# A backward pass with an S4 layer and a gated feed-forward net: parameter-gradient blocks with finer due times, their stores on GpSimd's queue, and the input gradient stored from ScalarE's queue

## The chip, the cores and the metric

The kernel runs on one core of a Trainium2 chip. The metric is the device time of one execution in microseconds (us). A core has five engines with a queue of instructions each: TensorE (PE, with its weight loads shown apart as PEld), VectorE (DVE), ScalarE (ACT), GpSimd (POOL) and SyncE (SP). A queue is worked in order, so an instruction that waits holds up all behind it. SP, ACT and POOL also issue DMA transfers between DRAM and the on-chip memory (SBUF); in the profile such issues carry the names SPq, ACTq and POOLq.

## The reference

The forward function normalises `A_u` (2048 rows of 576 channels) and feeds the result to two branches, an S4 convolution and a SwiGLU net with 4608 hidden channels; the output combines them. The kernel returns the output and the gradients of all inputs.

```python
x = A_u
xn = _layernorm(x, axis=-1)
s = _A_ref(xn, A_re, A_im, B_re, B_im, C_re, C_im, log_dt, Dskip)   # S4 convolution
g = _silu(_B_ref(xn, B_w1, B_w3, B_w2))                             # gated net
return x + s * g
...
dt = exp(log_dt); logdA = dt * (A_re + 1j * A_im); dB = dt * (B_re + 1j * B_im)
K[d, l] = real(sum_n C[d, n] * exp(logdA[d, n] * l) * dB[d, n])     # kernel of the convolution
y = irfft(rfft(pad(u)) * rfft(pad(K))) + u * Dskip
```

Outputs 0 and 1 are the result and the gradient of `A_u` (2048 x 576); outputs 2 to 7 are the gradients of A, B and C, real and imaginary parts (576 x 128 each); output 8 is the gradient of `log_dt` (576 numbers), output 9 that of `Dskip`; 10 to 12 are the weight gradients of the net.

## The kernel before

The program is one straight line of instructions for each engine. The forward pass comes first; `backward` (L1126) lays out the rest in stages that overlap: the backward convolution (`ssm_bwd_conv`), the parameter gradients (`ssm_bwd_params`, then `phase5_final`), the weight gradients of the net in 18 groups (`phase6_group`), and last the input gradient (`phase6_inputs`).

**What sets the order.** A planner writes the queue of each engine when the program is built. `at(us)` (L83) gives the instructions that follow a due time; when several instructions of an engine could run, the planner puts the one with the earliest due time first. It works with its own estimates of when things are ready, and once written the order is fixed. Buffers of a pool are reused in turn: a tile from a pool with three buffers waits until the tile three before it has been read for the last time. In `backward` the numbers are T0 = 700, TG = 36, TQ = 75, TC = 14, TX = 18, so the input gradient's tile i is due at 1348 + 18 i.

**Parameter gradients.** `param_chunk` (L1016) works through 36 chunks of 16 channels: PE multiplies into PSUM tiles `et_ps` (L1026), DVE multiplies by `pz` (L1033) and reduces into `S_all` (L1037). Its loads are issued on SP (L1008, L1013, and the transposing load at L1178). `phase5_final` (L1041) then takes the 576 channels in five blocks of 128 (the last has 64). For each block PE transposes four pieces of `S_all` (L1056), ACT copies them to `ST` (L1058), and DVE computes `W` (L314 to L321), `grho` and `gth` (L1067 to L1073), the sums for the gradient of `log_dt` (L1081 to L1097), and the gradients of B and C (L1101 to L1106). Six results of a block are scaled into tiles `gout` (L1076, L1108, L1111), of which there are three buffers, and stored with `self.dma` (L77, the issue itself is L81), which takes SP and ACT in turn. The memory of this step is that of the chunks' buffers, so it begins when the last chunk is done. After the last block the sums go out to output 8 in two stores on SP (L1119, L1121): the first writes 512 numbers of 2 bytes one by one, since neighbouring numbers lie in different partitions.

**Input gradient.** `phase6_inputs` (L1287) takes 16 tiles of 128 rows. For each tile SP loads two transposed operands, `ggc` and `guc` (L1178), which have two buffers each; PE runs 144 matmuls (L1316) into two PSUM halves `px`, also with two buffers; DVE adds the convolution's part into `gx` (L1326), which frees `px`; then `ln_bwd_tile` (L1356) takes the gradient through the layer norm on ACT (L1365) and DVE (L1368 to L1377), and the result `o1` is stored by `self.dma` (L1379), on SP and ACT in turn. ACT also issues the loads of `gxs` and `go` (L1322, L1324).

Of the kernel before, what the change touches and what calls it, by code (L numbers as in the profile page):

```python
# [16 lines left out]
P = 128  # L17
# [43 lines left out]
class K:  # L61
# [840 lines left out]
    def ssm_bwd_params(self, T0, TC, T2, S_all, ps):  # L902
        cfg = self.cfg
        D, LT = cfg.D, cfg.LT
        with self.tc.tile_pool(name="g_k", bufs=1, side="right") as gkp, self.tc.tile_pool(name="g_q", bufs=2, side="right") as qp:
            gz = []
            for i in range(3):
                z = gkp.tile([P, 2, 2, 2, 16, LT], BF16, name=f"gz{i}")
                self.nc.gpsimd.memset(z[:], 0.0)
                gz.append(z)  # L910
            NCH = D // 16
            AHEAD = 2
            q = []
            when = lambda c: T0 + TC * c + (40 if T0 + TC * c > T2 - 30 else 0)
            for ch in range(NCH + AHEAD):
                if ch < NCH:
                    self.at(when(ch - AHEAD))
                    q.append(self.param_load(ch, gz[ch % 3], qp))
                if ch >= AHEAD:
                    self.at(when(ch - AHEAD))  # L920
                    self.param_chunk(ch - AHEAD, q.pop(0), S_all, qp, ps)
# [119 lines left out]
    def phase5_final(self, out, big, S_all, ps2, T, TX):  # L1041
        nc, cfg = self.nc, self.cfg
        D, DT, N = cfg.D, cfg.DT, cfg.N
# [3 lines left out]
        pp = out.enter_context(self.tc.tile_pool(name="gfp", bufs=1, side="right"))  # L1047
        if True:
            self.load_rates(pp)
            glogdt = big.tile([P, DT], FP32, name="glogdt")  # L1050
            nc.vector.memset(glogdt[:], 0.0)
            for c, (do, dsz) in enumerate(cfg.dch):
                self.at(T + TX * c)
                pt = ps2.tile([P, 4, N], FP32, name="et_ps")
                for kd in range(4):
                    nc.tensor.transpose(pt[0:dsz, kd, :], S_all[:, kd, do:do + dsz], self.ident_f[:])  # L1056
                ST = fp.tile([P, 4, N], FP32, name="ST")
                nc.scalar.copy(out=ST[0:dsz], in_=pt[0:dsz])  # L1058
                v = slice(0, dsz)
                S1r, S2r, S1i, S2i = ST[v, 0, :], ST[v, 1, :], ST[v, 2, :], ST[v, 3, :]  # L1060
                Wr_t, Wi_t = self.compute_W(fp, c, dsz)
                Wr, Wi = Wr_t[v], Wi_t[v]
                dtc = self.dt_col[v, c:c + 1]
                grho = fp.tile([P, N], FP32, name="grho")
                gth = fp.tile([P, N], FP32, name="gth")
                t1 = fp.tile([P, N], FP32, name="ft1")
                nc.vector.tensor_tensor(out=grho[v], in0=Wr, in1=S2r, op=ALU.mult)  # L1067
                nc.vector.tensor_tensor(out=t1[v], in0=Wi, in1=S2i, op=ALU.mult)
                nc.vector.tensor_tensor(out=grho[v], in0=grho[v], in1=t1[v], op=ALU.subtract)
                nc.vector.tensor_tensor(out=gth[v], in0=Wr, in1=S2i, op=ALU.mult)  # L1070
                nc.vector.tensor_tensor(out=t1[v], in0=Wi, in1=S2r, op=ALU.mult)
                nc.vector.tensor_tensor(out=gth[v], in0=gth[v], in1=t1[v], op=ALU.add)
                nc.vector.tensor_scalar(out=gth[v], in0=gth[v], scalar1=-1.0, scalar2=None, op0=ALU.mult)  # L1073
                for src, oname in ((grho, "out_2"), (gth, "out_3")):
                    ob = fo.tile([P, N], BF16, name="gout")
                    nc.vector.tensor_scalar(out=ob[v], in0=src[v], scalar1=dtc, scalar2=None, op0=ALU.mult)  # L1076
                    self.dma(aps[oname][do:do + dsz, :], ob[v])
                acc1 = fp.tile([P, 1], FP32, name="acc1")
                acc2 = fp.tile([P, 1], FP32, name="acc2")
                junk = fp.tile([P, N], FP32, name="junk")  # L1080
                nc.vector.tensor_tensor_reduce(out=junk[v], in0=grho[v], in1=self.A_re[v, c, :], scale=1.0, scalar=0.0,  # L1081
                                               op0=ALU.mult, op1=ALU.add, accum_out=acc1[v])
                nc.vector.tensor_tensor_reduce(out=junk[v], in0=gth[v], in1=self.A_im[v, c, :], scale=1.0, scalar=0.0,
                                               op0=ALU.mult, op1=ALU.add, accum_out=acc2[v])
                nc.vector.tensor_tensor(out=acc1[v], in0=acc1[v], in1=acc2[v], op=ALU.add)
                acc3 = fp.tile([P, 1], FP32, name="acc3")
                acc4 = fp.tile([P, 1], FP32, name="acc4")
                nc.vector.tensor_tensor_reduce(out=junk[v], in0=S1r, in1=Wr, scale=1.0, scalar=0.0,
                                               op0=ALU.mult, op1=ALU.add, accum_out=acc3[v])
                nc.vector.tensor_tensor_reduce(out=junk[v], in0=S1i, in1=Wi, scale=1.0, scalar=0.0,  # L1090
                                               op0=ALU.mult, op1=ALU.add, accum_out=acc4[v])
                nc.vector.tensor_tensor(out=acc3[v], in0=acc3[v], in1=acc4[v], op=ALU.subtract)
                rdt = fp.tile([P, 1], FP32, name="rdt")
                nc.vector.reciprocal(out=rdt[v], in_=dtc)
                nc.vector.tensor_tensor(out=acc3[v], in0=acc3[v], in1=rdt[v], op=ALU.mult)
                nc.vector.tensor_tensor(out=acc1[v], in0=acc1[v], in1=acc3[v], op=ALU.add)
                nc.vector.tensor_tensor(out=glogdt[v, c:c + 1], in0=acc1[v], in1=dtc, op=ALU.mult)  # L1097
                for (Xr, Xi, on_r, on_i) in ((self.B_re, self.B_im, "out_6", "out_7"), (self.C_re, self.C_im, "out_4", "out_5")):
                    gr = fp.tile([P, N], FP32, name="gr")
                    gi_ = fp.tile([P, N], FP32, name="gi")  # L1100
                    nc.vector.tensor_tensor(out=gr[v], in0=S1r, in1=Xr[v, c, :], op=ALU.mult)  # L1101
                    nc.vector.tensor_tensor(out=t1[v], in0=S1i, in1=Xi[v, c, :], op=ALU.mult)
                    nc.vector.tensor_tensor(out=gr[v], in0=gr[v], in1=t1[v], op=ALU.subtract)
                    nc.vector.tensor_tensor(out=gi_[v], in0=S1r, in1=Xi[v, c, :], op=ALU.mult)
                    nc.vector.tensor_tensor(out=t1[v], in0=S1i, in1=Xr[v, c, :], op=ALU.mult)
                    nc.vector.tensor_tensor(out=gi_[v], in0=gi_[v], in1=t1[v], op=ALU.add)  # L1106
                    ob = fo.tile([P, N], BF16, name="gout")
                    nc.vector.tensor_scalar(out=ob[v], in0=gr[v], scalar1=dtc, scalar2=None, op0=ALU.mult)  # L1108
                    self.dma(aps[on_r][do:do + dsz, :], ob[v])
                    ob2 = fo.tile([P, N], BF16, name="gout")  # L1110
                    nc.vector.tensor_scalar(out=ob2[v], in0=gi_[v], scalar1=dtc, scalar2=-1.0, op0=ALU.mult, op1=ALU.mult)  # L1111
                    self.dma(aps[on_i][do:do + dsz, :], ob2[v])
            gl_bf = big.tile([P, DT], BF16, name="gl_bf")
            nc.vector.tensor_copy(out=gl_bf[:], in_=glogdt[:])
            nfull = D // P
            rem = D - nfull * P
            with nc.allow_non_contiguous_dma(reason="small vector store"):
                if nfull > 0:
                    nc.sync.dma_start(out=aps["out_8"][0:nfull * P].rearrange("(c p) -> p c", p=P), in_=gl_bf[:, 0:nfull])  # L1119
                if rem > 0:  # L1120
                    nc.sync.dma_start(out=aps["out_8"][nfull * P:D].rearrange("(p o) -> p o", o=1),  # L1121
                                      in_=gl_bf[0:rem, nfull:nfull + 1])
# [3 lines left out]
    def backward(self, T0, TG, TQ, TC, TX, gctx, mats):  # L1126
        nc, cfg = self.nc, self.cfg
        D, L, LT, F, FT = cfg.D, cfg.L, cfg.LT, cfg.F, cfg.FT
# [8 lines left out]
        with ExitStack() as out:  # L1137
# [7 lines left out]
            ps = out.enter_context(pool(name="b_ps", bufs=3, space=PS, side="right"))  # L1145
# [6 lines left out]
            T1 = T0 + 4 * TQ  # L1152
            self.ssm_bwd_params(T1, TC, T2, S_all, ps)
            self.at(T1 + TC * D // 16)
            self.phase5_final(out, fix, S_all, ps, T1 + TC * D // 16, TX)
            cur = self.phase6_load(0, T0 - TG, TG, wp, inp)
            for gi in range(NG):
                nxt = self.phase6_load(gi + 1, T0 + TG * gi, TG, wp, inp) if gi + 1 < NG else None
# [197 lines left out]
    def ln_bwd_tile(self, sb, sm, gx, i, go_t):  # L1356
# [19 lines left out]
        o1 = sb.tile([P, D], BF16, name="o1")  # L1376
        nc.vector.scalar_tensor_tensor(out=o1[:], in0=u[:], scalar=self.rstd[:, i:i + 1], in1=go_t[:],  # L1377
                                       op0=ALU.mult, op1=ALU.add)
        self.dma(out1[i * P:(i + 1) * P, :], o1[:])  # L1379


# [99 lines left out]
```

## Time and profile before

| | |
|---|---|
| median of 13 runs | 2059.11 us (2043.48 to 2103.01) |
| profiled execution | 2061.33 us, of which the span from first to last instruction is 2059.6 us |
| PE busy | 1789.9 us, 87% of the span |
| DVE busy | 1501.9 us, 73% |
| ACT busy | 968.4 us, 47% |
| POOL busy | 510.1 us, 25%; none after 1684 us |
| mean granted TensorE clock | 0.958 |

Times in the profile count from the span's start. The chain that ended last is followed back from the last instruction: each step is the work, or the wait, that released the next one. In a timeline, a bracket after a line tells how long the engine had been idle and what released it. The granted clock is the share of full speed that TensorE was allowed. `gout`, `o`, `gl_bf` and so on are the program's tile names with numbers left out (`out_dram` stands for any output).

### The profile page before, as it was taken

To read this page: it belongs to the slowest core of one execution; us is meant where nothing else is said; L and a number is where in the kernel's file an instruction comes from. 1 tells how busy PE (TensorE), PEld (TensorE's weight loads), DVE (VectorE), ACT (ScalarE), POOL (GpSimd) and SP (SyncE) were. 2 spreads that over 40 slices of the span, in tenths; PEclk is the share of its full clock that TensorE was granted. 3 is DMA by queue.
4 is the path that set the end of the run, shared out by engine and by line. 5 is a ranking of instruction groups with operands and counts; after the bars stand their busy time and mean duration, and the time that the engine had idled before them with its cause. 6 is when DMAs were issued, how large, how long until landed. Compare 5 with 4: busy or idle time off the path is not lost. (4 is left out here: it accounts for less than half of the span.)

```text
span 2059.6 us, 40511 instructions
## 1 busy us (share of the span) xinstructions
PE 1789.9 (87%) x16214; PEld 1246.7 (61%) x16214; DVE 1501.9 (73%) x2616; ACT 968.4 (47%) x1733; POOL 510.1 (25%) x682
## 2 busy tenths in 40 slices
PE   2888988989899699989999999897996994899985
PEld 1443333335454477777777777675775773677764
DVE  7459999998783456569695878586995865388681
ACT  1968888886456311474747565343543410000000
POOL 6016566662123011212122212322231210000000
PEclk9899999999999899999999999998998997999998
DMA  6678788877578998646463645999889899999773
GB/s 174 242 271 291 272 281 276 280 266 256 181 265 197 197 208 189 181 125 175 135 204 115 191 142 155 235 242 210 228 204 166 216 216 192 196 218 231 169 146 41
DMA packets 551981, 421.29 MB, mean 205 GB/s; under 512 B 415472, under 2 KB 482224, under 8 KB 547184
## 3 DMA queue, kind: packets, MB, share of 16 engines
q1 hardware_dynamic: 488096, 254.56, 52.0%
q0 software_dynamic: 39056, 147.49, 22.5%
q10 hardware_dynamic: 24640, 16.65, 3.2%
q8 instruction: 127, 2.08, 0.4%
q14 instruction: 62, 0.51, 0.1%
HBM read 135.96 MB, written 196.27 MB: 161 GB/s over the span
## 5 line engine op out<-in xcount | busy, mean ns | idle before, releaser
L1033 DVE TENSOR_TENSOR pr_q<-et_ps,pz 128x512 f32<-128x512 f32 x288 | 186.6, 684 | 77.1 <-PE et_ps L1026 70.3
L1272 PEld LDWEIGHTS <-xn_bf 128*128 128x128 bf16 x2304 | 224.3, 98 | 29.6 <-issue 2.9
L768 PEld LDWEIGHTS <-xnT 128*128 128x128 bf16 x1152 | 101.6, 98 | 168.6 <-issue 71.8
L1037 DVE TENSOR_REDUCE S_all<-pr_q 128x16 f32<-128x1024 f32 x144 | 175.1, 1216 | 2.1
L1225 PE MATMUL ph<-w2T,goT 128*128 128x256 bf16 x1152 | 173.1, 281 | 2.0 <-DVE e L840 2.0
L1253 PE MATMUL pgw<-go_o,h_n 128*128 128x288 bf16 x1152 | 163.7, 292 | 0.0
L768 PE MATMUL pg<-wmB_w,xnT 128*128 128x512 bf16 x576 | 160.2, 387 | 2.9 <-ACT g_t L777 2.0
L1316 PEld LDWEIGHTS <-guc 128*128 128x128 bf16 x1152 | 114.4, 100 | 77.3 <-DMA guc<-GU_dram 28.0
L1365 ACT ACTIVATE t<-gx 128x576 f32<-128x576 f32 x16 | 10.9, 683 | 314.6 <-DVE gx L1326 262.4
L768 PE MATMUL pu<-wmB_w,xnT 128*128 128x512 bf16 x576 | 152.7, 382 | 0.0
L499 POOL COPY pz_k<-p_k 128x256 bf16<-128x256 bf16 x144 | 138.7, 1006 | 46.6 <-issue 37.1
L831 PE MATMUL po<-w2g,hc 128*128 128x288 bf16 x1152 | 147.5, 291 | 1.3 <-ACT u_t L778 1.3
L1274 ACT CAST gw<-pgw 128x256 bf16<-128x256 f32 x144 | 54.5, 379 | 197.3 <-PE pgw L1272 196.5
L1316 PEld LDWEIGHTS <-ggc 128*128 128x128 bf16 x1152 | 114.6, 100 | 42.5 <-DMA ggc<-GG_dram 12.2
L1272 PE MATMUL pgw<-gu_n,xn_bf 128*128 128x256 bf16 x1152 | 132.9, 272 | 1.6 <-ACT gw L1257 1.1
L1316 PE MATMUL px<-wTA,guc 128*128 128x288 bf16 x512 | 110.5, 298 | 26.6 <-DMA guc<-GU_dram 26.6
L831 PEld LDWEIGHTS <-hc 128*128 128x128 bf16 x1152 | 113.2, 99 | 32.6 <-issue 1.7
L1253 PEld LDWEIGHTS <-h_n 128*128 128x128 bf16 x1152 | 112.7, 100 | 28.6
L1272 PE MATMUL pgw<-gg_n,xn_bf 128*128 128x256 bf16 x1152 | 129.4, 273 | 0.0
L1225 PEld LDWEIGHTS <-goT 128*128 128x128 bf16 x1152 | 101.6, 100 | 44.4 <-issue 14.8
L1316 PE MATMUL px<-wTA,ggc 128*128 128x288 bf16 x512 | 110.9, 297 | 17.9 <-DMA ggc<-GG_dram 12.1
L1228 ACT CAST gh<-ph 128x512 bf16<-128x512 f32 x144 | 82.2, 604 | 81.7 <-PE ph L1225 51.6
(321 smaller groups left out, 4179.8 us busy)
## 6 DMA issues: line engine op xcount, KB each, us to landing
G_dram<-g_t POOLq DMA_DIRECT2D x72, 256.0 KB, 4.0
U_dram<-u_t POOLq DMA_DIRECT2D x72, 256.0 KB, 3.6
H_dram<-h_t SPq DMA_DIRECT2D x72, 256.0 KB, 3.4
Q_dram<-q_k SPq DMA_DIRECT2D x36, 512.0 KB, 3.4
gg_n<-G_dram POOLq DMA_DIRECT2D x18, 1024.0 KB, 5.8
h_n<-U_dram POOLq DMA_DIRECT2D x18, 1024.0 KB, 8.3
GU_dram<-gu_n POOLq DMA_DIRECT2D x72, 256.0 KB, 4.3
GG_dram<-gg_n POOLq DMA_DIRECT2D x72, 256.0 KB, 5.6
```

The source lines that it names most:

```text
L499: nc.gpsimd.tensor_copy(out=pz[:, g, h, 1:3], in_=pv[:, g, h])
L768: nc.tensor.matmul(pt[:], lhsT=xnT[:, c, ts], rhs=wm[w][:, c, :], start=(c == 0 and not first), stop=(c == nfull - 1 and first))
L831: nc.tensor.matmul(po_[:, pi_, 0:pw], lhsT=hc[:, fi, :], rhs=w2[fi][:, po:po + pw], start=(fi == 0), stop=(fi == FT - 1))
L1033: nc.vector.tensor_tensor(out=pr[:, r].rearrange("p k m a -> p m k a"), in0=T[h][:, r][:, None].to_broadcast([P, 2, 4, 2, AV]), in1=pz[:, ...
L1037: nc.vector.tensor_reduce(out=S_all[:, :, d0:d0 + 4].rearrange("p (s k) d -> p k s d", k=2), in_=pr[:].rearrange("p r k (s d) a -> p k s d ...
L1225: nc.tensor.matmul(ph[j][:, k, :], lhsT=lw, rhs=rh, start=(n == 0), stop=(n == nfull))
L1228: nc.scalar.copy(out=gh[:, j], in_=ph[j][:])
L1253: nc.tensor.matmul(pgw[pi_][:, 0:pw], lhsT=hn[:, tt, fl * P:(fl + 1) * P], rhs=go_o[:, tt, po:po + pw], start=(tt == 0), stop=(tt == LT - 1))
L1272: nc.tensor.matmul(pw_[:, 0:FG], lhsT=self.xn_bf[:, tt, c * P:(c + 1) * P], rhs=nat[:, tt, :], start=(tt == 0), stop=(tt == LT - 1))
L1274: nc.scalar.copy(out=gw[:, c, :], in_=pw_[:, 0:FG])
L1316: nc.tensor.matmul(px[pi_][:, 0:pw], lhsT=act[:, fi, :], rhs=wT[p][ai][:, fi - f0, po:po + pw], start=(fi == 0 and ai == 0), stop=(fi == F ...
L1365: nc.scalar.activation(out=t[:], in_=g, func=ACT.Copy, scale=-invD, accum_out=mg[:])
```

## The change

The five blocks of `phase5_final` get later and closer due times (start 1514 instead of 1504, distance 16 instead of 18), and each block's parts get due times of their own within the distance. While `phase5_final` is laid out, `self.dma` issues on GpSimd's queue; after it only `ln_bwd_tile` would use `self.dma`, and that store is now issued from ScalarE's queue. The stores to output 8 stay on SP. The first edit adds zero to a due time.

```diff
@@ ssm_bwd_params
-                    self.at(when(ch - AHEAD))
+                    self.at(when(ch - AHEAD) + 0 * TC)
@@ phase5_final
             self.load_rates(pp)
+            self.dma_engines = [nc.gpsimd]
...
                 S1r, S2r, S1i, S2i = ST[v, 0, :], ST[v, 1, :], ST[v, 2, :], ST[v, 3, :]
+                self.at(T + TX * (c + 0.12))
                 Wr_t, Wi_t = self.compute_W(fp, c, dsz)
                 Wr, Wi = Wr_t[v], Wi_t[v]
                 dtc = self.dt_col[v, c:c + 1]
+                self.at(T + TX * (c + 0.3))
                 grho = fp.tile([P, N], FP32, name="grho")
...
+                self.at(T + TX * (c + 0.45))
                 for src, oname in ((grho, "out_2"), (gth, "out_3")):
...
+                self.at(T + TX * (c + 0.55))
                 acc1 = fp.tile([P, 1], FP32, name="acc1")
...
+                self.at(T + TX * (c + 0.65))
                 acc3 = fp.tile([P, 1], FP32, name="acc3")
...
                 for (Xr, Xi, on_r, on_i) in (...):
+                    self.at(T + TX * (c + (0.8 if on_r == "out_6" else 0.9)))
@@ backward
-            self.phase5_final(out, fix, S_all, ps, T1 + TC * D // 16, TX)
+            self.phase5_final(out, fix, S_all, ps, T1 + TC * D // 16 + 10, 16)
@@ ln_bwd_tile
-        self.dma(out1[i * P:(i + 1) * P, :], o1[:])
+        nc.scalar.dma_start(out=out1[i * P:(i + 1) * P, :], in_=o1[:])
```

## The prediction

> **What bounds the kernel now.** I read the page first: PE is busy 87% of the span, and the loss in the second half sits at its ends. The chain that ended last, in order of time (start, us, step), gives the tail:
>
> ```profile
> 1977.14 0.38 DVE gx L1326
> 1977.56 31.30 PE px L1316 x235
> 2008.86 23.80 DMA guc<-GU_dram
> 2032.71 19.65 PE px L1316 x141
> 2052.38 0.83 DVE gx L1326 x2
> ```
>
> PE computes the input gradient tile by tile (144 matmuls on L1316 each); the chain leaves it twice, for DVE's gx and for a load of 23.8 us. Busy times by stretch (PE, PEld, DVE, ACT, POOL, then clock, DMA share, GB/s):
>
> ```profile
> 1932.50:1971.70 39.20, 38.90 (x324) 30.84 (x322) 31.20 (x129) 3.12 (x6) 0.00 (x0) 1.00 0.77 167
> 1971.70:1977.50 5.80, 0.01 (x1) 0.00 (x0) 5.80 (x38) 0.00 (x0) 0.00 (x0) 0.85 0.16 35
> 1977.50:2015.40 37.90, 37.84 (x289) 29.32 (x289) 26.91 (x124) 2.91 (x7) 0.00 (x0) 0.93 0.83 147
> 2015.40:2032.70 17.30, 0.30 (x3) 0.00 (x0) 3.87 (x8) 0.78 (x2) 0.00 (x0) 0.64 0.87 88
> 2032.70:2052.40 19.70, 19.69 (x142) 14.79 (x142) 0.02 (x1) 0.00 (x0) 0.00 (x0) 0.89 0.00 1
> ```
>
> PE is full to 1971.7, idle 5.8 us while DVE is full, full for tiles 13 and 14, idle 17.3 us, then runs tile 15 alone. After each hole the granted clock is below 1.00. Why the load is late stands in SP's queue, from the timeline:
>
> ```profile
> 2000.27 0.52 SPq L81 DMA_DIRECT2D out_dram<-gout  x1
> 2000.88 5.41 SPq L1178 DMA_TRANSPOSE ggc<-GG_dram  x1
> 2006.39 1.18 SPq L81 DMA_DIRECT2D out_dram<-gout  x2
> 2007.62 0.58 SPq L1119 DMA_DIRECT2D out_dram<-gl_bf  x1
> 2008.26 0.50 SPq L1121 DMA_DIRECT2D out_dram<-gl_bf  x1
> 2008.86 21.05 SPq L1178 DMA_TRANSPOSE guc<-GU_dram  x1
> ```
>
> and in the transfers of the last 60 us (last number: us from issue to landing):
>
> ```profile
> go<-in_grad_out_dram ACTq DMA_DIRECT2D x1, 144.0 KB, 20.5
> out_dram<-gl_bf SPq DMA_DIRECT2D x1, 1.0 KB, 18.6
> guc<-GU_dram SPq DMA_TRANSPOSE x1, 23.8
> ```
>
> Tile 15's second load stands behind out_8's store: 512 elements of 2 bytes scattered over DRAM, 18.6 us for 1 KB. In 2010 to 2027 the DMA moves 22 to 27 GB/s; the transpose lands 6.5 us after that store. The end of this kernel is set by the queue order of the parameter gradients' final step.
>
> **The change, part by part.**
>
> *No-ops.* `+ 0*TC` adds zero. load_rates keeps SP and ACT, since the engine list is changed after it. The first blocks still start when the last parameter chunk is reduced (1945.9): their memory is that of the chunk buffers.
>
> *Due times.* Blocks were due at 1504, 1522, 1540, 1558, 1576, whole; tiles 11, 12, 13, 14, 15 are due at 1546, 1564, 1582, 1600, 1618. DVE follows that: blocks 0 to 2, then tile 11's gx at 1977.05, although PE finished tile 11 at 1953. Tile 13 needs tile 11's PSUM buffer, hence the hole. Now blocks start at 1514, 1530, 1546, 1562, 1578, and a block's parts are spread over the next 14.4. Tile 11 (1546) comes ahead of block 2's arithmetic (1547.9), tile 12 at block 3's start, tile 13 inside block 4. Block work is 37 instructions of 0.20 us between starts plus six of 0.07, 7.8 us. Blocks 0 and 1 then end at 1950.2 + 15.6 + store waits of 3 to 7 = 1969 to 1973, against 1971.7 when PE wants the buffer. I take 1 us of hole instead of 5.85, and with it most of the clock loss: chain view 31.30 us for 235 matmuls, against 28.8 at the 17.64 us for 144 of the tiles before. Gain 4.9 + 2.5 = **7 us**.
>
> *Stores of the blocks to POOL.* 30 issues leave SP and ACT (15 each). On SP they stood between the loads: tile 14's ggc went out at 1976.4, 4.7 us after its buffer was free. Nothing else is in POOL's queue after 1684, so nothing waits behind them. The cost is the slot: three gout buffers, and DVE waits for a store to land. Nearest rows, same 32 KB:
>
> ```profile
> out_dram<-gout ACTq DMA_DIRECT2D x12, 32.0 KB, 1.7
> out_dram<-gout SPq DMA_DIRECT2D x12, 32.0 KB, 2.2
> out_dram<-gw13t POOLq DMA_DIRECT2D x36, 32.0 KB, 5.1
> ```
>
> In a block only the sixth store meets a slot still in flight, written some 2 us earlier; by the POOL row (0.55 us issue on POOL, 5.1 landing) that is 3.6 us a block, 18 in all, against 9.2 us waited now. From below: the fastest POOL store took 3.6 us, about 2 us a block, 10 in all. I take +5. It lies on DVE, not PE: each tile has 17.6 us of slack before its PSUM buffer is wanted. So 0 on PE; if that cover is gone, up to +9 us.
>
> Two rules of the Trainium skill speak against this edit. "SBUF — State Buffer", the box on the "DVE blocks DMA" trap: a DVE operation in a two-port mode keeps GpSimd from writing descriptors, and a 0.62 us DMA became 3.1 us. By that price 30 stores take 93 us of POOL and the last lands past 2045: about +10 us on the end. The trace has the case: POOL's small gw13t stores issued in 541 to 563 ns, all 36 of them, with DVE running beside. I go by the row: 30 x 0.55 = 17 us on an idle queue. "DMA: Bandwidth & Descriptors", "Issuing engines are not separate DMA queues": another issuing engine saves only sequencer time, since all share 16 DMA engines. By it the slow out_8 store hurts whatever is in flight, on any queue; the row agrees (go, on ACT's queue, took 20.5 us). So the gain must come from the store's place in time.
>
> *Place of the out_8 store.* It stays on SP, due 1592.4 instead of 1576. The planner takes ready work only: tile 15's loads (1618) are ready when PE ends tile 13, out_8 when DVE ends block 4's sums. Before, the two met: the store slipped between ggc and guc. Now tile 13 ends earlier (1971.7 + 17.7 = 1989.4, instead of about 1997) and block 4 later: DVE has 39 us of blocks + 3 x 3.7 us of tiles + 10 to 18 us of waits after 1950.2, so gl_bf at 2007 to 2018. Even at 5.4 us each both loads are issued by about 2000. I expect ggc, guc, then out_8: hole 17.0 gone, and tile 15 back from 19.65 us for 141 to 17.3. Gain **19 us**. The store then ends at 2026 to 2037, beside PE.
>
> *out_1 from ACT.* Eight stores leave SP, at 0.53 us. Around 1787 and 1830 SP is the chain (its transposes release PE), so 0 to 1.2 us gained; all later ones are covered by a full PE. On ACT the store waits for DVE's o, about 4 us after gx; behind it stand the go load of two tiles on, which needs the same o, and ACT's own step 17 us later: 0. Cover gone (DVE late in a block), the ST copy behind it waits some 4 us. Against that, a reshuffle of SP's chunk loads costs 0 to 3. I take 0.
>
> *Sum.* PE's end 2052.4 - 7 - 19 = 2026.4; after it the same 7.2 us: 2033.6, with out_8's landing about as late (2026 to 2037) and the last o store sharing engines with it, +1. Span 2034.6 against 2059.6, i.e. -25. The profiled execution took 2061.3, the median is 2059.1: **2034 us** by the median.
>
> **Rivals.**
>
> 1. *out_8 still splits the pair.* For: the planner's times put them within some 4 us before, and my order has about that margin. gl_bf at 2007 to 2018, guc lands 25.1 us after as now (2007.62 to 2032.71), tile 15 19.7, tail 7.2: 2059 to 2070. Middle 2061, same to slightly slower.
> 2. *Slower: out_8 ahead of both loads.* SP then waits for gl_bf and both transposes stand behind the slow store: 25.1 + 5.4 us after gl_bf = 2038 to 2049, + 26.9 = 2064 to 2075. It decides once DVE ends block 4's sums before PE ends tile 13. Against it: 39 us of block work cannot end by 1990.
> 3. *Slots.* POOL stores slow DVE so that gx is late twice: +9, and out_8 ends near 2040: 2045.
> 4. *It does nothing here*: DVE still puts blocks before gx and the order of SP is as now, 2059. Against: the due times cross.
>
> **How the numbers follow.** Forecast 0.62, own range 2023 to 2045; rival 1 0.14; rival 2 0.10; rival 3 0.08; rival 4 0.06. The runs shown scatter by 8 us (half the distance between their quartiles, 2048.7 and 2065.1). So 2023 is 2034 less 1 of hole, 1 of shared engines, 1.2 from SP's o stores and 8 of scatter; 2045 is out_8 landing last, at 2037, with the same 8. The range runs from 2023 to 2062: it takes in rivals 3 and 4 and most of 1, and leaves out 2 in 10, chiefly rival 2. About 0.5% (10 us) is what a measurement of this kernel tells from no change. Faster: forecast and most of rival 3, 0.68. Same: rival 4 and half of 1, 0.14. Slower: rival 2, half of 1 and the rest, 0.18.
>
> **What would show it.** Right: no idle of PE above 2 us between tiles 11 and 15; SP's queue with ggc and guc adjacent for tile 15 and gl_bf after them; tile 11's gx before 1972 if the chunks end at 1946; POOL issues of 0.55 us; clock 1.00 to the end. Wrong: a guc landing above 20 us, gout waits above 20 us on DVE, POOL issues of some us, or a changed order of the chunk loads before 1860 that costs PE more than 3 us.

## The result, and the profile after

The changed kernel takes 2027.82 us (median of 11 runs, 2014.8 to 2067.83), the kernel before, beside it, 2059.08 us. The ratio is 0.9887 with a 95% interval of 0.9856 to 0.9918, that is 17 to 30 us less. The ratios here and below compare fast runs alone, so the medians, which take in slow ones too, lie 31.3 us apart; of the profiles in the table below, those of "before, out_8 after both loads" and "changed, out_1 on ACT and SP" are of slow runs. The profiled execution took 2032.57 us, of which the span is 2030.7.

The chain that ended last, of the changed kernel (start, us, step):

```profile
1952.29 0.44 PE et_ps L1057 x4
1952.72 17.64 PE px L1323 x144
1970.36 0.44 PE et_ps L1057 x4
1970.80 52.81 PE px L1323 x431
2023.64 0.83 DVE gx L1333 x2
```

L1323, L1333 and L1185 are the lines that were L1316, L1326 and L1178. The chain no longer leaves PE for DVE or a load: tile 12 takes 17.64 us for its 144 matmuls, and tiles 13 to 15 follow at once, 431 in 52.81 us, which is 17.64 us for 144 again. So the clock lost nothing either, as the busy times by stretch show (PE, PEld, DVE, ACT, POOL, clock, DMA share, GB/s):

```profile
1932.50:1971.00 38.50, 38.20 (x313) 30.31 (x312) 30.25 (x123) 3.78 (x8) 6.34 (x12) 1.00 0.85 172
1971.00:1989.00 18.00, 18.00 (x149) 14.38 (x147) 14.66 (x70) 1.35 (x3) 3.37 (x7) 1.00 0.83 193
1989.00:2006.00 17.00, 17.00 (x141) 13.58 (x139) 14.38 (x82) 0.78 (x2) 4.44 (x9) 1.00 0.79 179
2006.00:2023.70 17.70, 17.70 (x145) 13.91 (x143) 7.20 (x23) 0.78 (x2) 2.02 (x4) 1.00 0.21 38
```

SP's queue, from the timeline:

```profile
1988.23 4.74 SPq L1185 DMA_TRANSPOSE ggc<-GG_dram  x1
1993.07 5.15 SPq L1185 DMA_TRANSPOSE guc<-GU_dram  x1
2009.13 0.39 SPq L1126 DMA_DIRECT2D out_dram<-gl_bf  x1
2009.57 0.52 SPq L1128 DMA_DIRECT2D out_dram<-gl_bf  x1
```

Both loads of the last tile are out before the stores to output 8: the second load's issue ends at 1998.22, 10.9 us ahead of them. The transfers after 1970 us (last number: us to landing):

```profile
out_dram<-gout POOLq DMA_DIRECT2D x14, 32.0 KB, 3.8
ggc<-GG_dram SPq DMA_TRANSPOSE x2, 8.5
guc<-GU_dram SPq DMA_TRANSPOSE x2, 8.5
out_dram<-gl_bf SPq DMA_DIRECT2D x1, 0.1 KB, 15.4
```

A load of `guc` lands in 8.5 us, where the last one took 23.8. The stores to output 8 are still slow: the second lands 15.4 us after its issue, at 2025.0, beside PE's last matmuls and the start of the last layer norm. DVE's waits for a free `gout` buffer (a slot) from 1930 us on (us in all, times, longest), and the POOL issues in the list of groups (count | busy us, mean ns | idle time before them, and what ended most of it):

```profile
DVE gout L1118 <- DMA out_dram<-gout: 9.3, 5, 3.3
```

```profile
L81 POOL DMA_DIRECT2D out_dram<-gout x30 | 16.2, 539 | 304.4 <-DVE gth L1076 266.3 <-DVE gth L1075 12.2 <-DVE gr L1110 5.3
```

### The profile page after: what moved, and what is told of

Read it like the earlier page. It is cut to its first block, busy times and chain, and to the rows that moved or that the text cites. A ratio compares the mean times of both kernels' runs of the same rounds, so it can differ in the third digit from the quotient of the medians.

```text
span 2030.7 us, 40521 instructions
## 1 busy us (share of the span) xinstructions
PE 1803.8 (89%) x16214; PEld 1249.6 (62%) x16214; DVE 1503.9 (74%) x2616; ACT 969.2 (48%) x1733; POOL 519.6 (26%) x712
## 5 line engine op out<-in xcount | busy, mean ns | idle before, releaser
L1232 PE MATMUL ph<-w2T,goT 128*128 128x256 bf16 x1152 | 180.5, 289 | 3.7 <-DVE e L840 2.0
L768 PE MATMUL pg<-wmB_w,xnT 128*128 128x512 bf16 x576 | 165.9, 398 | 2.9 <-ACT g_t L777 2.0
L768 PE MATMUL pu<-wmB_w,xnT 128*128 128x512 bf16 x576 | 158.0, 392 | 3.6 <-ACT u_t L778 3.6
L499 POOL COPY pz_k<-p_k 128x256 bf16<-128x256 bf16 x144 | 131.7, 957 | 48.7 <-issue 39.6
L1323 PEld LDWEIGHTS <-guc 128*128 128x128 bf16 x1152 | 113.1, 99 | 47.1 <-issue 7.7
L1372 ACT ACTIVATE t<-gx 128x576 f32<-128x576 f32 x16 | 10.9, 684 | 274.5 <-DVE gx L1333 274.4
L1323 PEld LDWEIGHTS <-ggc 128*128 128x128 bf16 x1152 | 113.1, 99 | 40.3 <-DMA ggc<-GG_dram 12.0
L1323 PE MATMUL px<-wTA,ggc 128*128 128x288 bf16 x512 | 106.9, 289 | 11.8 <-DMA ggc<-GG_dram 11.8
L1238 DVE TENSOR_TENSOR gu_n<-gh,gu_n 128x1024 bf16<-128x1024 bf16 x72 | 49.4, 686 | 90.2 <-ACT gh L1235 90.2
```

The costliest lines, as they stand in the source:

```text
L499: nc.gpsimd.tensor_copy(out=pz[:, g, h, 1:3], in_=pv[:, g, h])
L768: nc.tensor.matmul(pt[:], lhsT=xnT[:, c, ts], rhs=wm[w][:, c, :], start=(c == 0 and not first), stop=(c == nfull - 1 and first))
L1232: nc.tensor.matmul(ph[j][:, k, :], lhsT=lw, rhs=rh, start=(n == 0), stop=(n == nfull))
L1323: nc.tensor.matmul(px[pi_][:, 0:pw], lhsT=act[:, fi, :], rhs=wT[p][ai][:, fi - f0, po:po + pw], start=(fi == 0 and ai == 0), stop=(fi == F ...
```

## The experiments

The profiles in the table reach the final step at times from 1924.6 to 1953.9 us, and single times of one kernel differ by as much (ten of the changed kernel's eleven lie between 2014.8 and 2041.44 us). So profiles, one for each row, are compared over **the stretch** from SP's first load of rates (`A_re`) to the end of the span: 113.7 us before (1945.90 to 2059.6), 85.7 after (1945.00 to 2030.7). "gx hole" is PE's wait for DVE's `gx`, "load hole" its wait for `ggc` or `guc`, both in the stretch.

| kernel | gx hole | load hole | stretch | time, ratio to before |
|---|---|---|---|---|
| before | 5.9 | 17.0 | 113.7 | 1 |
| before, out_8 after both loads | 5.6 | 2.1 | 96.7 | 0.9907 (0.9873 to 0.9941) |
| before, out_8 from POOL | 5.7 | 15.3 | 111.6 | 0.9947 (0.9899 to 0.9995) |
| before, out_8 as rows | 5.8 | 0 (and 4.6 of its own) | 101.8 | 0.9934 (0.9899 to 0.9969) |
| before, new due times alone | 0 | 5.5 | 93.3 | 0.9841 (0.9785 to 0.9897) |
| changed | 0 | 0 | 85.7 | 0.9887 (0.9856 to 0.9918) |
| changed, again | 1.7 | 0 | 87.8 | 0.9865 (0.9795 to 0.9934) |
| changed, old due times | 10.5 | 12.9 | 113.4 | 1.0025 (0.9981 to 1.0070) |
| the same, out_8 after both loads | 8.8 | 0.9 | 98.2 | 0.9929 (0.9896 to 0.9962) |
| changed, block stores on SP and ACT | 0 | 8.9 | 97.8 | 0.9864 (0.9804 to 0.9925) |
| changed, second slow store | 11.9 | 0 | 100.7 | 1.0000 (0.9963 to 1.0037) |
| changed, out_1 on ACT and SP | 0 | 0.3 | 86.2 | 0.9878 (0.9842 to 0.9913) |

**The place of out_8, alone.** The kernel before, with a due time of 1630 for the two stores, and nothing else:

```diff
+            self.at(1630)
             with nc.allow_non_contiguous_dma(reason="small vector store"):
...
```

> The kernel before with one edit: the two stores to output 8 are due at 1630, after tile 15's loads (1618), so that they stand behind guc on SP; nothing else moves. Theory (the place of the slow store makes the second hole): guc goes out at about 2007.6 and lands 8 to 10 us later at 2016 to 2017, hole 1 to 2 us instead of 17.0, the last tile about 17.5 us instead of 19.65; the hole of 5.85 us stays. 17 us faster than before, a ratio of 0.992. Rival (guc is slow there for another reason, or the gain comes from the stores leaving SP): guc still lands over 20 us after its issue and the time is that of before, ratio 1.000.

The timeline of SP in this kernel:

```profile
2009.43 5.33 SPq L1179 DMA_TRANSPOSE ggc<-GG_dram  x1
2014.85 1.18 SPq L81 DMA_DIRECT2D out_dram<-gout  x2
2016.13 4.98 SPq L1179 DMA_TRANSPOSE guc<-GU_dram  x1
2021.16 0.58 SPq L1120 DMA_DIRECT2D out_dram<-gl_bf  x1
```

and the end of its chain:

```profile
2016.13 8.13 DMA guc<-GU_dram
2024.30 19.13 PE px L1317 x141
```

`guc` is issued 6.7 us after `ggc`, block stores still between them, and lands in 8.13 us. The load hole falls from 17.0 to 2.1 us, the stretch by 17.0. The gx hole stays, as it should. By the stretch, the place of one store is the larger part of the gain, 17.0 of 28.0 us.

**The same store from another queue.** The kernel before, out_8 issued by GpSimd: it is then behind nothing and in front of nothing on SP.

```diff
-                    nc.sync.dma_start(out=aps["out_8"][0:nfull * P].rearrange("(c p) -> p c", p=P), in_=gl_bf[:, 0:nfull])
+                    nc.gpsimd.dma_start(out=aps["out_8"][0:nfull * P].rearrange("(c p) -> p c", p=P), in_=gl_bf[:, 0:nfull])
...
-                    nc.sync.dma_start(out=aps["out_8"][nfull * P:D].rearrange("(p o) -> p o", o=1),
+                    nc.gpsimd.dma_start(out=aps["out_8"][nfull * P:D].rearrange("(p o) -> p o", o=1),
```

> The kernel before with one edit: the two stores to output 8 are issued from GpSimd's queue, at the same place in time (about 2004 to 2007). It parts two readings of the 18.6 us. If the transposing load waits because it stands behind the slow store in SP's ring: it now lands 8 to 10 us after its issue at about 2007, hole under 3 us, ratio 0.992. If the 16 DMA engines are shared, so that the slow writes hold up any transfer in flight: guc still takes 16 to 22 us, the hole is 10 to 15 us and the ratio 0.996 to 1.000.

The last `ggc` and the store in the timelines of SP and POOL, and the transfers in the last 56 us:

```profile
1981.16 5.46 SPq L1178 DMA_TRANSPOSE ggc<-GG_dram  x1
1984.43 0.77 POOL L1119 DMA_DIRECT2D out_dram<-gl_bf  x1 [320.96 <-DVE gl_bf L1114]
```

```profile
ggc<-GG_dram SPq DMA_TRANSPOSE x1, 21.8
out_dram<-gl_bf POOLq DMA_DIRECT2D x1, 1.0 KB, 18.1
guc<-GU_dram SPq DMA_TRANSPOSE x1, 21.6
```

Now both loads are slow, `ggc` too, though it was issued 3.3 us before the store. PE waits 9.4 and 5.9 us, and the stretch gains only 2.1. The holes, 15.3 us in all, are a little over the 10 to 15 expected, and the ratio is a little better than expected, with an interval that reaches into the expected range. So it is not the order on SP's queue alone that delays a load, but the store's transfers while they are in flight, whichever queue issues them. The DMA engines are not idle meanwhile: in the kernel before, from 2018 to 2027 us, their busy share is 0.89 while they move 26 GB/s. Whether the engines or the DRAM behind them hold the loads up, no run here parts.

**The same store, made cheap, in the same place.** The kernel before, the sums turned to a row by TensorE, so that out_8 is five pieces of 256 or 128 bytes instead of 576 of 2 bytes:

```diff
-            gl_bf = big.tile([P, DT], BF16, name="gl_bf")
-            nc.vector.tensor_copy(out=gl_bf[:], in_=glogdt[:])
+            pg8 = ps2.tile([P, 4, N], FP32, name="et_ps")
+            nc.tensor.transpose(pg8[0:DT, 0, :], glogdt[:], self.ident_f[:])
+            gl_row = big.tile([DT, P], BF16, name="gl_row")
+            nc.scalar.copy(out=gl_row[:], in_=pg8[0:DT, 0, :])
...
+            nc.sync.dma_start(out=aps["out_8"][0:nfull * P].rearrange("(c p) -> c p", p=P), in_=gl_row[0:nfull, :])
```

> The kernel before, with out_8 turned into rows by a TensorE transpose and stored by five descriptors (four of 256 bytes and one of 128) in the same two stores at the same place between the last ggc and the last guc on SP's queue. Theory (the price of the 576 two-byte writes is the cause, not the place of the stores): guc lands 8 to 11 us after its issue, the hole ahead of the last tile is 0 to 4 us, the first hole stays at 4 to 6 us, the stretch from the first load of rates to the end of the span is 95 to 99 us and the time 0.990 to 0.993 of before. Rival (SP's queue waiting for out_8's sum is the cause): guc still starts late and the hole stays over 9 us, the stretch 108 to 114 us and the time 0.997 to 1.003.

SP's queue in this kernel, and the load in its list of transfers:

```profile
1979.54 5.31 SPq L1174 DMA_TRANSPOSE ggc<-GG_dram  x1
1984.95 1.18 SPq L81 DMA_DIRECT2D out_dram<-gout  x2
1986.22 0.44 SPq L1119 DMA_DIRECT2D out_dram<-gl_row  x1
1986.72 0.23 SPq L1120 DMA_DIRECT2D out_dram<-gl_row  x1
1987.17 4.63 SPq L1174 DMA_TRANSPOSE guc<-GU_dram  x1
```

```profile
guc<-GU_dram SPq DMA_TRANSPOSE x1, 7.7
```

The order is that of before, and the same 1.1 KB are stored, yet `guc` holds SP for 4.63 us instead of 21.05 and lands in 7.7 instead of 23.8; PE waits for no load. The stretch, 101.8, is above the 95 to 99 expected, since the added transpose stands in PE's queue ahead of tile 14 and waits 4.6 us for the sums, a wait that the edit itself brought. Without it the stretch would be 97.2, by subtraction. The time agrees: the interval of the ratio takes in the value of the late store. With the two kernels above this settles the cause: the 576 pieces of 2 bytes, whatever queue issues them, while they are in flight. Whether their size or their number counts is not parted, since five pieces are both longer and fewer.

**A second slow store.** The changed kernel, with 512 numbers of tile 12's `o1` also written 2 bytes at a time to a scratch buffer, ahead of the last tile's loads. No output changes.

```diff
+                if i == LT - 1:
+                    self.nat_transpose(acts[0][:], self.GG_dram[i])
...
+                        nc.sync.dma_start(out=self.two_dram[:].rearrange("(c p) -> p c", p=P), in_=self.o_keep[:, 0:4])
+                    self.nat_transpose(acts[1][:], self.GU_dram[i])
```

> The changed kernel with a second store of 512 numbers of 2 bytes (four columns of tile 12's result, to scratch memory), which stands on SP ahead of tile 15's ggc and guc. Theory (the slow store's place is what counts): SP reaches it once tile 12's result is there, some 45 us after the first load of the rates; guc lands over 20 us later, PE has a hole of 10 to 14 us before tile 15 and 2 us of low clock after it: the stretch from the first load of the rates to the end is 98 to 102 us instead of 85.7, ratio to before 0.993 to 0.997. Rival (the loads were late for other reasons): under 3 us more, ratio 0.987 to 0.990.

The planner put it ahead of both loads. SP's queue, and then DVE's timeline:

```profile
1987.33 0.37 SPq L1362 DMA_DIRECT2D two_dram<-o  x1
1987.82 19.83 SPq L1186 DMA_TRANSPOSE ggc<-GG_dram  x1
```

```profile
2007.69 0.29 DVE L1118 TENSOR_SCALAR gout<-gi,dt_col 128x128 bf16<-128x128 f32 x1 [16.44 <-DMA out_dram<-gout]
```

and a block store in the chain that ended last:

```profile
1989.16 21.77 DMA out_dram<-gout
```

The stretch grew by 15.0 us to 100.7, inside what was expected, but not by the way expected. `ggc` held SP for 19.8 us, and that block store on POOL's queue took 21.77 us to land instead of some 3.5; DVE waited 16.4 us for one slot and 2.0 for the next, `gx` was late, and PE stood 11.9 us for that. The slow store hits stores of other queues as well. The time's ratio of 1.0000 is 0.6% above what the stretch alone would give (2059 - 13.0 = 0.9937), and its interval leaves that out: this difference of 13 us is not explained.

**The due times, undone.** The changed kernel without the parts' due times, blocks at the old start and distance, all else as changed:

```diff
-                self.at(T + TX * (c + 0.12))
...
-                    self.at(T + TX * (c + (0.8 if on_r == "out_6" else 0.9)))
...
-            self.phase5_final(out, fix, S_all, ps, T1 + TC * D // 16 + 10, 16)
+            self.phase5_final(out, fix, S_all, ps, T1 + TC * D // 16, TX)
```

> The changed kernel with the due times of before (blocks whole, 1504 and every 18); stores of the blocks stay on GpSimd's queue, the input gradient's on ScalarE's. In this queue order output 8 stands between ggc and guc of tile 15 again. Theory (due times make both gains): both holes are back, about 5 us and 13 to 17 us, time within 4 us of before, ratio 0.998 to 1.002. Rival (the gain comes from the stores leaving SP and ACT): most of the gain stays, ratio 0.990.

PE's timeline:

```profile
1964.79 0.40 PE L1317 MATMUL px<-wTA,ggc 128*128 128x288 bf16 x1 [10.50 <-DVE gx L1327]
2015.18 0.66 PE L1317 MATMUL px<-wTA,guc 128*128 128x288 bf16 x2 [12.95 <-DMA guc<-GU_dram]
```

Both holes are back, and time and stretch are those of before. The store to output 8 stands between the last `ggc` and `guc` again. The moves to POOL and ACT bring nothing without the due times. The gx hole, 10.5 us, is larger than the 5 expected; in part these are DVE's waits for slots ahead of that `gx`, 5.2 us here and 2.9 before.

**Old due times, out_8 after the loads.** The last kernel with the edit of the first experiment.

> The changed kernel with the due times of the parameter-gradient pieces as they were before, and out_8's two stores put after both loads of the last tile. Measured from the first load of rates to the end of the span, the changed kernel has 85.7 us and the one with the old due times alone 113.4 us, with holes on PE of 10.5 us (ahead of the tile whose gx waits behind the pieces) and 12.95 us (for the last guc). Theory: the two holes have two causes; the second goes with the place of out_8 (guc lands 8 to 10 us after its issue), the first stays at 9 to 12 us, and the stretch is 97 to 101 us: 0.994 of before, between 0.991 and 0.998. Rival: with out_8 out of the way the pieces fit in DVE's slack, the first hole falls under 4 us and the stretch is 86 to 91 us, 0.989 of before.

Its list of what PE waited for in the stretch (total us, times, longest):

```profile
PE px L1318 <- DVE gx L1328: 8.8, 1, 8.8
PE px L1318 <- DMA guc<-GU_dram: 0.9, 1, 0.9
```

The two holes have two causes. The place gives 113.4 - 98.2 = 15.2 us; going on to the changed kernel, 98.2 - 85.7 = 12.5 us come with the finer due times, chiefly from `gx` ahead of the blocks. But one expectation failed: the last `guc` was to land in 8 to 10 us. It was issued 5.3 us ahead of the store (2004.39 and 2009.64), and the chain has

```profile
2004.39 14.23 DMA guc<-GU_dram
```

so a load that stands ahead of the store is not yet safe. In the late store of the first experiment the gap was as short (5.0 us) and `guc` landed in 8.13 us; in the changed kernel it is 16.1 us (1993.07 to 2009.13). How large it has to be is open.

**The block stores, and the input gradient's.** The changed kernel with the blocks' stores on SP and ACT in turn:

```diff
-            self.dma_engines = [nc.gpsimd]
```

> The changed kernel with the blocks' stores back on SP and ACT in turn; due times and the input gradient's store as changed. In this queue order output 8 stands behind guc of tile 15, but six to seven gout stores stand between tile 13's and tile 14's loads, and one each before ggc and guc of tile 15. By the prediction's sum (moving the stores is worth 0 on PE): time of the changed kernel within 3 us, ratio to before 0.987 to 0.990. Rival (a store that waits for DVE holds up the loads behind it on SP): ggc of tile 15 cannot go before block 4's first results at about 2001, guc at 2006, landing 2015, when PE wants it at 2006: hole about 9 us plus 2 us of clock, ratio 0.993 to 0.995.

PE's timeline:

```profile
1979.59 0.42 PE L1322 MATMUL px<-wTA,guc 128*128 128x288 bf16 x2 [2.16 <-DMA guc<-GU_dram]
2004.18 0.66 PE L1322 MATMUL px<-wTA,guc 128*128 128x288 bf16 x2 [6.78 <-DMA guc<-GU_dram]
```

Out_8 goes out after both loads here too (2001.45), so this is another delay: stores stand before and between the loads on SP and wait there for DVE. The last `guc` also took 11.9 us to land (1992.24 to 2004.13), with the store to output 8 going out in its last 3 us; what share of the 6.78 us that has is not parted. The stretch is 12.1 us longer than the changed kernel's. The time, from four runs, does not show it. So the due times were tried alone, out_1 on SP and ACT as well, beside the changed kernel on the same chip:

```diff
+                self.at(T + TX * (c + 0.12))
...
+                    self.at(T + TX * (c + (0.8 if on_r == "out_6" else 0.9)))
...
-            self.phase5_final(out, fix, S_all, ps, T1 + TC * D // 16, TX)
+            self.phase5_final(out, fix, S_all, ps, T1 + TC * D // 16 + 10, 16)
```

> The kernel before with the new due times alone: the stores of the blocks and the input gradient alternate on SP and ACT as before. With out_1 on ACT as well, the stretch from the first load of rates to the end of the span had 97.8 us against 85.7 of the changed kernel and 113.7 before, but four times of that kernel gave a ratio of 0.986, too few to tell. Theory A (block stores between the loads on SP hold these up): a last guc that goes out behind stores of block 4, holes for guc of 5 to 12 us in all, a stretch of 96 to 101 us and a time 0.6 to 0.8% below before, 10 to 12 us above the changed kernel. Theory B (that profile was chance): no hole for guc over 2 us, a stretch of 86 to 90 us and a time within 0.3% of the changed kernel's.

> The changed kernel itself, beside the due times alone on the same chip. Theory A: no hole of PE after tile 11, a stretch of 85 to 87 us, 0.9887 of before (0.986 to 0.992), and the due times alone 10 to 12 us slower. Theory B: the two within 6 us of each other. By either, the stretch repeats within 1 us in a second profile, while the start of the stretch may lie up to 20 us elsewhere.

SP's queue with the due times alone:

```profile
1980.35 9.32 SPq L81 DMA_DIRECT2D out_dram<-gout  x4
1989.76 4.58 SPq L1184 DMA_TRANSPOSE ggc<-GG_dram  x1
1994.44 0.54 SPq L81 DMA_DIRECT2D out_dram<-gout  x1
1995.08 7.16 SPq L1184 DMA_TRANSPOSE guc<-GU_dram  x1
```

Four stores of blocks keep SP for 9.32 us ahead of the last `ggc`, and PE waits 2.6 and 2.9 us for `guc`. The stretch is 93.3 us, between the two expectations. The medians are 2030.44 us for the due times alone and 2032.86 for the changed kernel, six runs each, whose ratios have intervals of 1.1 and 1.4% of the time. So the due times alone bring all of the gain that these times can show; that the stores on POOL save 5.5 to 8.9 us of holes is seen in the profiles only. The second profile of the changed kernel has a stretch of 87.8 us, 2.1 above the first: the "within 1 us" expected was too narrow.

For the input gradient's stores, the changed kernel with out_1 on ACT and SP in turn:

```diff
-        nc.scalar.dma_start(out=out1[i * P:(i + 1) * P, :], in_=o1[:])
+        (nc.scalar, nc.sync)[i % 2].dma_start(out=out1[i * P:(i + 1) * P, :], in_=o1[:])
```

> The changed kernel with the input gradient's stores on ScalarE's and SyncE's queue in turn, as before. Theory (that edit is worth 0 to 1.2 us): no hole of PE above 2 us between tiles 11 and 15, the stretch from the first load of the rates to the end 85 to 88 us, ratio to before as for the changed kernel, 0.986 to 0.991. Rival (SP waits for DVE's result before a load and is late with it): a hole of 3 us or more before one of tiles 13 to 15, stretch 89 us or more.

No hole above 0.3 us, a stretch of 86.2 us, a ratio of 0.9878: this edit is worth nothing that either measure shows. The margin is gone, though: the chain runs through the store on SP (1980.31), the `ggc` behind it (1980.76) and `guc` (1986.53), which lands just as PE wants it.

**Two tries to go further.** PE still waits 11.8 us for a `ggc` before tile 2 (to 1754.11 us), 190 us ahead of the stretch. One try made the loads of tiles 2 to 15 due a tile earlier, the other gave them a third buffer:

```diff
-                self.at(T2 + TX * i)
+                self.at(T2 + TX * (i - 1))
                 acts, px = alloc(i)
                 load(acts, i, 0, FT)
+                self.at(T2 + TX * i)
...
-        with self.tc.tile_pool(name="x_in", bufs=2) as inp, \
+        with self.tc.tile_pool(name="x_in", bufs=3) as inp, \
```

> An attempt at a faster version: the changed kernel with the loads of the input gradient's tiles 2 to 15 due one tile earlier, so that SP puts them ahead of the parameter chunks' loads. It aims at the holes of 11.8 and 3.1 us that PE has before tile 2, where SP works through chunk loads first. If SP's order makes them: 5 to 8 us less than the changed kernel, ratio to before 0.984 to 0.986. Rival: the chunks are late instead, the last one and with it the blocks and output 8 end later, and the time is that of the changed kernel or more.

> A second attempt: the changed kernel with three buffers for ggc and guc instead of two, so that a tile's load does not wait for the tile two before it. If the holes of 11.8 and 3.1 us before tile 2 come from the buffer: both go, and the waits for guc later in the stage with them, 10 to 15 us less than the changed kernel, ratio to before 0.980 to 0.984. Rival (SP's transposing loads are the limit in that stretch, buffer or not): the hole shrinks by under 4 us or moves to tile 3, ratio 0.986 to 0.989.

The earlier due times changed nothing: 11.9 us of wait for that `ggc`, a stretch of 85.7 us, a ratio of 0.9874 (0.9811 to 0.9937), which is the changed kernel's. The third buffer made it slower, 1.0360 (1.0291 to 1.0430): from 1800 to 1900 us PE was busy 45.5 us at a clock of 0.62, since the chunks' products then stood in PE's queue without input-gradient matmuls between them (the first of these in that window starts at 1871.1), and over the whole run PE waited 92.5 us for `pr_q` in 39 waits, against 30.7 in 10. That the third buffer's memory is what pushed the tiles behind the chunks fits, but was only argued.

## Why the prediction was right, point by point

2034 us was predicted, 2027.82 measured; the gain predicted was 25 us, the measured one is 17 to 30 by the ratio, and 28.0 in the stretch of the profiles.

- **What bounds the kernel** (the place of a 2-byte store in SP's order): right as to the store and its place in time, shown by the three out_8 kernels. The queue order on SP only sets that time: issued from POOL at nearly the same moment, it was nearly as bad (15.3 us of holes against 17.0).
- **Due times** (7 us: hole 5.85 to 1, clock 2.5): right. Tile 11's second `gx` ended at 1969.8, 1 us before PE began tile 13 (1970.80), so 0 instead of 1 us is left (1.7 in the second profile), and the clock stayed at 1.00. In the context of the changed kernel they are worth more, 12.5 us, because there the old ones leave a hole of 8.8 to 10.5 us.
- **Place of out_8** (19 us): right in order, and near in size: the place alone gave 17.0 us in the kernel before and 15.2 with the stores on POOL. `gl_bf` was forecast for 2007 to 2018 (the terms given add up to 2010 to 2018) and its store went out at 2009.13; tile 13 was to end at 1989.4, and `ggc` went out at 1988.23 upon it. The second store landed at 2025.0, 15.8 us after the first one's issue and ahead of the 2026 to 2037 given, which rest on the 18.6 us that the first one took before. The 1 us for sharing engines with it did not appear: from PE's end to the end of the span it is 7.1 us (2023.64 to 2030.7) against 7.2 before.
- **Stores of the blocks to POOL** (+5 us on DVE, 0 on PE): the step that was mis-sized. DVE waited 9.3 us in all for slots, as before (9.2), not 10 to 18: a 32 KB store landed in 3.5 us (median over the stage), not the 5.1 of the row used. And the edit is not 0 on PE: I counted the loads as free to go in the place step and gave nothing for the queue that lets them. In the profiles, leaving those stores on SP costs 5.5 us of load holes with the due times alone and 8.9 with out_1 on ACT too. The bound "if that cover is gone, up to +9 us" was tried by the old due times: the gx hole grew from 5.9 to 8.8 and 10.5, so 3 to 5 us.
- **The two rules of the Trainium skill.** The 3.1 us of "SBUF — State Buffer" stand just behind the box on the trap, in "A bandwidth-pool intuition that's wrong", and are for a DVE `tensor_copy` beside the DMA; at that price 30 issues would have taken some 3.1 us each. They took 539 ns each with DVE 14.7 of 18.0 us busy beside them, so the row was the right guide. Whether any of that DVE work ran in the page's two-port mode the trace does not tell, so this does not test the page. "DMA: Bandwidth & Descriptors", "Issuing engines are not separate DMA queues", says that another issuing engine saves only sequencer time, and this case agrees: out_8 from POOL slowed both loads to over 21 us.
- **out_1 from ACT** (0): right, 86.2 against 85.7 us.
- **Sum.** Counted from the first load of rates, PE's end was to come at 80.5 us (2026.4 - 1945.9) and came at 78.6 (2023.64 - 1945.00). That the sum is so close is in part luck: the place gave 17.0 us, 2 less than forecast, and the rest of the change 11.0 (96.7 - 85.7), 4 more than the 7 forecast for the due times.
- **Rivals.** Rival 1 (out_8 splits the pair) is what the kernel with the old due times does, 1.0025. Rival 2 was tried by a like store: ahead of both loads it costs 15 us. Rival 3's late `gx` appeared there too, under the slow store, and with the old due times, but not in the changed kernel, for which it was put. Rival 4 did not occur.

What stays open: by the profiles the changed kernel should be 7.6 us (stretch) ahead of the due times alone, and the times are the other way, by 2.4 us (medians) or 5 us (ratios), with intervals too wide to call it a contradiction. Nor is it known why the second slow store cost 13 us more in time than in the stretch.

## What to carry to other kernels

A store of a kilobyte in 2-byte pieces can take longer than a load of 1.2 MB (128 rows of 4608 numbers of 2 bytes; 15 to 19 against 8.5 us here) and hold that load up; look in the list of transfers for a landing time out of proportion to its bytes, and then for what is in flight beside it on any queue. Move such a store to a moment without urgent loads, also none just ahead of it, or make its pieces longer and fewer; another queue did not help here. Where a planner writes the queues, a large step's due time belongs on its parts, so that a short instruction for which the bounding engine waits can go between them.

## What was not expected of the hardware

- The 576 pieces of 2 bytes of output 8 took 14.7 to 18.6 us to land, and what was in flight beside them from SP, ACT or POOL could land 13 to 18 us late: `go` in 20.5 us (median 5.8), a 32 KB store on POOL in 21.8 (usually 3.5), `ggc` and `guc` in 21.6 to 24.4 (usually 7 to 10). Even a load issued 3.3 us earlier was caught. As five pieces of 128 to 256 bytes the same output delayed nothing.
- A hole of PE costs more than its length: after the hole of 5.8 us in the kernel with out_8 as rows the granted clock was 0.81 in the hole and 0.89 in the 21 us after it; in the changed kernel, without holes, it was 1.00 to the end.
- From the input gradient's first load to the first load of rates the kernels with block stores on POOL took 265 to 270 us, those without 270 to 275, one profile each and the third buffer's kernel left out, though those stores come only later. The stretch leaves this out. Why is open.
